# GpSimd adds the shared unit's softmax weights to each head's sums; one of four rounds of denominator products is left out

## The chip, the cores and the metric

The kernel runs on one core of a Trainium2 chip. The metric is the device time in microseconds (us); of several runs the median is given. Engines are named as the profile names them: PE is TensorE (matrix products), PEld its weight loads, DVE is VectorE, ACT is ScalarE, POOL is GpSimd, SP is SyncE, which here only issues loads.

## What is computed

Attention over 8 batches and 12 heads of 448 tokens and 64 columns, with a soft cap on the scores, and behind it a layer of 8 experts, of which each token uses one.

```python
scores = scale * np.matmul(q, k.transpose(0, 1, 3, 2))
scores = cap * np.tanh(scores / cap)
scores = scores - np.max(scores, axis=-1, keepdims=True)
attn = np.exp(scores)
attn = attn / (np.sum(attn, axis=-1, keepdims=True) + 1e-09)
x = np.matmul(attn, v)            # then heads side by side: 3584 tokens x 768
...
logits = x @ w_gate + modality_bias[modality_id]
e_idx = np.argmax(logits, axis=1)
...
h = np.maximum(x[mask] @ w1[e], 0.0)
out[mask] = gate_w[mask, None] * (h @ w2[e])
```

## The kernel before

**Pairs and units.** The heads of a batch are taken two at a time: 6 pairs a batch, 48 pairs in all, numbered g = 0 to 47. The 448 keys of each head are cut into three units of 128 keys of its own and a rest of 64. The rests of the two heads share one more unit, in which head 0 has partitions 0 to 63 and head 1 partitions 64 to 127. So a pair has 2 x 3 own units, whose softmax weights are the tile `pt` (128 keys by 6 by 448 queries), and one shared unit, whose weights are the tile `sh` (128 by 448). Keys stand on the partitions, queries along the row.

**One iteration.** `attention` runs g from 0 to 48. An iteration computes the scores of pair g in four steps (`scores`, L452, three products for each unit out of `hi` and `lo`, the two parts of the keys and queries that `prep` makes on DVE), ACT makes tanh (`th`, L454) and exponential (`pt` or `sh`, L456) out of them. In step 1, for pair g - 1: DVE adds the three own units of each head into `tot` (128 by 2 heads by 448; L555 and L556), and PE multiplies the own units with the values into `xT` (`weigh_own`, L461). In step 3 the shared unit's product (`weigh_shared`, L466) closes `xT`, and DVE copies it out of PSUM (L588). There is one `xT` buffer in PSUM, so `weigh_own` of the next iteration waits for that copy. The order on PE, and that of most DVE work, is the order in which the program is written; PE and DVE take one instruction after another.

**Denominators and gate logits.** Three pairs make a group h (`HB` = 3, 16 groups). The sum over keys, which is the denominator of the softmax, is itself a product: `sums` (L476) multiplies with the constant `pick`, which has a column of ones at row `GE` + j for head j. For each group it runs in four parts of three products each, all into one PSUM tile `glog`, with 32 rows for each pair:

| part | right-hand side | weights | what it adds |
|---|---|---|---|
| 0 | `tot` of head 0 | `pick[:, 0]` | the own keys of head 0 |
| 1 | `tot` of head 1 | `pick[:, 1]` | the own keys of head 1 |
| 2 | `sh` | `pick[:, 2]` | the shared unit, partitions 0 to 63 for head 0 and 64 to 127 for head 1 |
| 3 | `xT` copy | `wgt` | the unnormalized gate logits |

With r = (g - 4) mod 3, parts 0 and 1 run in the iterations with r = 0 (g = 4, 7, ... 46), parts 2 and 3 in those with r = 1 (g = 5, 8, ... 47), both in step 1 behind `weigh_own`; the last group's four parts run after the loop. Then DVE copies `glog` to `gl` (L480), PE turns it (`lt`, L488), and DVE divides (`logits`, L493 and L496). After every second group a batch is complete, and `route` picks each token's expert: DVE operations from L210 on, two small products in the next iteration (r = 2), then `rows` (L244, L247), `posf` and `pos` on DVE, and four indirect DMAs on POOL that put each token into the map `mapd` (L264).

**POOL.** GpSimd issues the stores of finished rows (`xd`, L517), those puts, the loads of the map (`mt`, L659) and the gathers of rows for an expert (`xg`, L666), and it has a small IOTA (`pay`, L255) that waits for the puts of the batch before to land. It does all of this in one queue, in order.

**The hand-over.** From g = 46 on the first expert's weights come in, and in the last iteration the first gathered rows (`xg`) are turned on PE (`ptr`, L702) in between. Behind the attention the products of the experts (L729 to L758) fill PE to the end.

**Buffers.** `tot` and `sh` have five buffers each (`HB + 2`), `pt` two.

Of the kernel before, what the change touches and what calls it, by code (L numbers as in the profile page):

```python
# [39 lines left out]
F32 = mybir.dt.float32  # L40
# [4 lines left out]
ALU = mybir.AluOpType  # L45
# [6 lines left out]
NP = H // 2  # L52
# [6 lines left out]
GW = 32  # L59
# [16 lines left out]
class Program:  # L76
# [7 lines left out]
    def pin(self, inst):  # L84
        return self.tc.keep_in_program_order(inst)
# [13 lines left out]
    def constants(self, cpool, dram):  # L99
        nc = self.nc  # L100
        self.xd = dram.tile([NT, DM], F32, name="xd")
        self.mapd = dram.tile([E * RG + W, 2], F32, name="mapd")
        self.metad = dram.tile([128, 4], I32, name="metad")

        self.ident = cpool.tile([128, 128], F32, name="ident")
        make_identity(nc, self.ident)
        self.identr = cpool.tile([128, 128], F32R, name="identr")
        nc.vector.tensor_copy(self.identr, self.ident)
        self.capt = cpool.tile([128, 1], F32, name="capt")
        nc.scalar.dma_start(self.capt, self.cap.unsqueeze(0).to_broadcast([128, 1]))  # L110
        self.flag = cpool.tile([1, 1], I32, name="flag")
        nc.vector.tensor_scalar(self.flag, self.capt[0:1], self.capt[0:1], CAP_FAST * CAP_FAST, op0=ALU.mult, op1=ALU.is_gt)
        self.cabs = cpool.tile([128, 1], F32, name="cabs")
        nc.vector.scalar_tensor_tensor(self.cabs, self.capt, -1.0, self.capt, op0=ALU.mult, op1=ALU.max)
        self.isc = cpool.tile([128, 1], F32, name="isc")
        nc.vector.reciprocal(self.isc, self.cabs)
        nc.vector.tensor_scalar(self.isc, self.isc, 0.125, None, op0=ALU.mult)


        act = cpool.tile([128, 1], F32, name="act")  # L120
        nc.scalar.activation(act, self.ident[:, 0:1], AF.Tanh)


        self.pick = cpool.tile([128, 3, GW], F32, name="pick")
        nc.vector.memset(self.pick, 0.0)
        for j in range(2):
            nc.vector.memset(self.pick[:, j, GE + j : GE + j + 1], 1.0)
            nc.vector.memset(self.pick[j * KR : (j + 1) * KR, 2, GE + j : GE + j + 1], 1.0)
        self.ones = cpool.tile([CP, 512], BF16, name="ones")
        nc.vector.memset(self.ones, 1.0)  # L130
        self.tri = cpool.tile([CP, CP], BF16, name="tri")
        nc.gpsimd.affine_select(
            self.tri, self.ones[:, :CP], pattern=[[1, CP]], compare_op=ALU.is_gt, fill=0.0, base=0, channel_multiplier=-1
        )
        self.desc = cpool.tile([128, E], F32, name="desc")
        nc.gpsimd.iota(self.desc, pattern=[[-1, E]], base=E, channel_multiplier=0, allow_small_or_imprecise_dtypes=True)
        self.region = cpool.tile([128, E], F32, name="region")
        nc.gpsimd.iota(self.region, pattern=[[RG, E]], base=0, channel_multiplier=0, allow_small_or_imprecise_dtypes=True)

        def table(name, shape, pattern, base=0, channel=0):  # L140
            t = cpool.tile(shape, F32, name=name)
            nc.gpsimd.iota(
                t, pattern=pattern, base=base, channel_multiplier=channel, allow_small_or_imprecise_dtypes=True
            )
            return t

        self.blkj = table("blkj", [128, E, RB], [[0, E], [1, RB]])
        self.blkr = table("blkr", [128, E, RB], [[RG, E], [W, RB]])
        self.blke = table("blke", [128, E, RB + 1], [[1, E], [0, RB + 1]])
        self.exp = table("exp", [128, E], [[1, E]])  # L150
        self.slot = table("slot", [128, 1], [[0, 1]], channel=1)

        self.acc = cpool.tile([CP, E], BF16, name="acc")
        nc.gpsimd.memset(self.acc, 0.0)
# [258 lines left out]
    def attention(self, qk, first, rp):  # L413
        tc, nc = self.tc, self.nc
        pe, pin = nc.tensor, self.pin
        with ExitStack() as st:
# [51 lines left out]
            def sums(h, part):  # L468

                if part == 0:  # L470
                    self.glog = ps_g.tile([128, 512], F32, name="glog")
                for t in range(HB):
                    xs_, tot, sh = kept[h * HB + t]
                    w = self.pick[:, part] if part < 3 else self.wgt[:, (h * HB + t) % NP]
                    rhs = (tot[:, 0], tot[:, 1], sh, xs_)[part]
                    pin(pe.matmul(self.glog[t * GW : (t + 1) * GW, :S], w, rhs, start=part == 0, stop=part == 3))  # L476

            def copy_sums():
                gl = xp.tile([HB * GW, S], F32, name="gl")
# [60 lines left out]
            for g in range(NG + 1):  # L540
# [4 lines left out]
                for step in range(C):  # L545
                    if step % 2 == 0 and g < NG:
                        scores(step, pt, sh, *cur[:2])
                        scores(step + 1, pt, sh, *cur[:2])
                    if step == 1:
                        if g + 1 < NG:  # L550
                            ready = prep(g + 1)
                        if g:
                            ppt, psh, pva = pend
                            tot = xp.tile([128, 2, S], F32, name="tot", bufs=HB + 2)
                            pin(nc.vector.tensor_tensor(tot, ppt[:, 0:2], ppt[:, 2:4], op=ALU.add))  # L555
                            pin(nc.vector.tensor_tensor(tot, tot, ppt[:, 4:6], op=ALU.add))  # L556
                            xT = ps_x.tile([128, 512], F32, name="xT")
                            weigh_own(xT, ppt, pva)

                        if g > HB:  # L560
                            h, r = divmod(g - HB - 1, HB)
                            if r < 2:
                                sums(h, 2 * r)
                                sums(h, 2 * r + 1)
                                if r:
                                    gl = copy_sums()
                    if step == 3:
                        if g in routing:
                            next(routing.pop(g), None)
                        if g == 3:  # L570
                            self.empty_map()
                        if g == 2:
                            self.gate_bias()

                        h, t = divmod(g - 2 * HB, HB)
                        if h >= 0 and (t == 0 or h < LAST):
                            if t == 0:
                                rec, xs = recs.pop(h), xp.tile([CP, C, HB * 128], F32, name="xs")
                            for u in (t,) if h < LAST else range(HB):
                                rows_out(h, u, xs, rec, h >= LAST)  # L580
                            if t == HB - 1 or h >= LAST:
                                store(h, xs)
                            if h == LAST:
                                meta = self.early_slot(self.cpool, self.ps_r)
                        if g:
                            weigh_shared(xT, psh, pva)
                            xs_ = xp.tile([128, S], F32, name="xT", bufs=2 * HB + 1)
                            pin(nc.vector.tensor_copy(xs_, xT[:, :S]))  # L588
                            kept[g - 1] = xs_, tot, psh
                        fetch(g + 2)  # L590
                        h, r = divmod(g - HB - 1, HB)
                        if h >= 0 and r == 1:
                            b = h // NH
                            if h % NH == 0:
                                lgs[b] = xp.tile([CP, C, H, E], F32, name="lg")
                            recs[h] = logits(h, by_token(gl), lgs[b])
                            if h % NH == NH - 1:
                                way = self.route(b, lgs[b], rp, self.ps_r)
                                next(way)
                                routing[g + 1] = way  # L600
                    for k in SPLITS.get((g, step), ()):
                        self.split_w(raws[k], self.w1s[k], pin=True)
                        if len(raws) < KC:
                            raws.append(self.load_raw(e, self.w1, len(raws), FF))
                    for k in MOVES.get((g, step), ()):
                        self.transpose(k, (ps_s, self.ps_r)[k % 2], ("sc", "small")[k % 2], busy=k < 2)
# [6 lines left out]
                    self.gather(early[1], known=NT - S)  # L613
            self.raws = [self.load_raw(e, self.w2, k, DM) for k in range(self.nstage)]
            h = NG // HB - 1
            for part in range(4):
                sums(h, part)
            rec = logits(h, by_token(copy_sums()), lgs[B - 1])
            way = self.route(B - 1, lgs[B - 1], rp, self.ps_r)
# [422 lines left out]
```

## Time and profile before

| | |
|---|---|
| median of three runs | 957.08 us (954.23 to 959.16) |
| the profiled execution | 955.14 us, its span 953.5 us |
| the attention | to about 421 us, at some 8 us a pair |
| the hand-over | some 400 to 425 us |
| products `glog` (L476), records x mean | `tot` 192 x 548 ns, `sh` 96 x 550 ns, `xT` 96 x 539 ns |
| additions for `tot` on DVE (L555, L556) | 48 x 1084 ns, 48 x 1092 ns |
| POOL busy | 131.6 us, 145 instructions |

One float32 product shows as two records on PE, so a part of `sums` (three products) shows as six. Records of neighbouring products overlap, so how long PE is taken is read from one start to the next. A row of the order of time has the start, the duration, the engine, the line, the operation with its tiles, and in brackets how long the engine stood idle ahead of it and for whom. A row of a group has the busy time in all and the mean of one in ns, then the idle time ahead of them. A row of a stage has the stage, its length, each engine's busy time, the granted clock and the DMA share.

### The profile page before, as it was taken

How to read it: one execution, taken by the hardware profiler on the slowest of the kernel's cores; microseconds unless marked ns; L12 is line 12 of the kernel's file. 1: busy time of each engine (PE TensorE's matmuls, PEld its weight loads, DVE VectorE, ACT ScalarE, POOL GpSimd, SP SyncE). 2: the span in 40 equal slices, each digit the busy share in tenths (PEclk: the TensorE clock that was granted, in tenths of full speed). 3: DMA queues.
4: the chain of work that ended last, by engine and by line, in shares of the span. 5: the costliest groups of instructions: out<-in, count | busy, mean ns of one | idle time of the engine just before them, and what ended most of it. 6: DMA issues, size and time to landing. Idle time of an engine off the chain costs nothing. (4 is left out here: it accounts for less than half of the span.)

```text
span 953.5 us, 14508 instructions
## 1 busy us (share of the span) xinstructions
PE 903.4 (95%) x5360; PEld 699.5 (73%) x5360; DVE 549.4 (58%) x940; ACT 558.5 (59%) x759; POOL 131.6 (14%) x145
## 2 busy tenths in 40 slices
PE   7999999999999999678899999999999999999997
PEld 3444445454545454258899999999999999998986
DVE  4777777777777778466444253343444443429662
ACT  6998888888888887603344343342444444336551
POOL 2002020202020202202420202020010202020100
PEclk9999999999999999978999999999999999999998
DMA  3433444453436343823863535455463635237660
GB/s 120 121 106 105 135 113 134 115 135 114 133 116 126 124 124 133 214 64 96 265 200 123 189 126 179 152 164 201 144 221 128 230 112 185 103 125 262 220 208 8
DMA packets 47178, 140.01 MB, mean 147 GB/s; under 512 B 8686, under 2 KB 9198, under 8 KB 47088
## 3 DMA queue, kind: packets, MB, share of 16 engines
q1 hardware_dynamic: 38000, 105.78, 36.2%
q0 software_dynamic: 8944, 33.10, 10.3%
q8 instruction: 47, 0.77, 0.3%
q14 instruction: 43, 0.35, 0.1%
q10 hardware_dynamic: 144, 0.00, 0.0%
HBM read 117.35 MB, written 22.69 MB: 147 GB/s over the span
## 5 line engine op out<-in xcount | busy, mean ns | idle before, releaser
L454 ACT ACTIVATE th<-sc,isc 128x896 f32<-128x896 f32 x192 | 168.7, 908 | 54.2 <-PE sc L452 54.1
L733 PE MATMUL ph<-x,al 128*128 128x384 f32 (+2 forms) x528 | 167.2, 317 | 0.0
L758 PE MATMUL py<-bh,hh 128*128 128x384 f32 x464 | 159.8, 344 | 4.3 <-ACT hh L739 4.3
L758 PE MATMUL py<-bl,hh 128*128 128x384 f32 x464 | 156.3, 337 | 0.0
L758 PE MATMUL py<-bh,hl 128*128 128x384 f32 x464 | 156.1, 337 | 0.0
L456 ACT ACTIVATE pt<-th,cabs 128x896 f32<-128x896 f32 x144 | 149.5, 1044 | 2.7
L729 PE MATMUL ph<-x,ah 128*128 128x384 f32 x384 | 129.9, 338 | 1.5 <-DVE hl L740 1.5
L730 PE MATMUL ph<-x,ah 128*128 128x384 f32 x384 | 129.0, 336 | 0.0
L461 PE MATMUL xT<-pt,va 128*64 128x448 f32 x576 | 119.7, 551 | 8.7 <-DVE xT L588 7.1
L683 DVE TENSOR_TENSOR bl<-raw,bh 128x768 fp32r<-128x768 f32 x88 | 81.3, 955 | 58.2 <-ACT bh L682 55.7
L682 ACT CAST bh<-raw 128x768 fp32r<-128x768 f32 x88 | 70.3, 839 | 68.0 <-DMA raw<-in_w_dram 55.3
L733 PEld LDWEIGHTS ph<-x,al 128*128 128x128 f32 x528 | 101.0, 191 | 0.0
L683 DVE TENSOR_TENSOR al<-raw,ah 128x1024 fp32r<-128x1024 f32 x66 | 78.8, 1222 | 27.8 <-ACT ah L682 27.3
L452 PEld LDWEIGHTS sc<-hi 64*128 64x128 f32 (+1 forms) x336 | 36.5, 187 | 77.7 <-ACT th L454 25.9
L763 ACT ACTIVATE ot<-py,mt 128x384 f32<-128x384 f32 x58 | 33.7, 581 | 99.2 <-PE py L758 51.8
L758 PEld LDWEIGHTS py<-bh,hh 128*128 128x128 f32 x464 | 87.8, 189 | 5.0 <-ACT hh L739 4.9
L712 DVE TENSOR_TENSOR x<-ptr,x 128x384 fp32r<-128x384 f32 (+2 forms) x66 | 32.7, 517 | 100.1 <-ACT x L711 97.0
L452 PE MATMUL sc<-hi 64*128 64x448 f32 (+1 forms) x336 | 86.9, 446 | 2.7 <-ACT th L454 2.1
L461 PEld LDWEIGHTS xT<-pt,va 128*64 128x64 f32 x576 | 37.5, 137 | 69.2 <-issue 45.4
L758 PEld LDWEIGHTS py<-bl,hh 128*128 128x128 f32 x464 | 87.9, 189 | 0.0
L758 PEld LDWEIGHTS py<-bh,hl 128*128 128x128 f32 x464 | 87.7, 189 | 0.1
L739 ACT ACTIVATE hh<-ph 128x384 fp32r<-128x384 f32 x64 | 30.4, 489 | 94.4 <-PE ph L733 94.4
(159 smaller groups left out, 1349.5 us busy)
## 6 DMA issues: line engine op xcount, KB each, us to landing
raw<-in_w_dram SPq DMA_DIRECT2D x66, 512.0 KB, 5.5
raw<-in_w_dram SPq DMA_DIRECT2D x88, 384.0 KB, 4.7
kq<-in_kq_dram SPq DMA_DIRECT2D x47, 480.0 KB
va<-in_v_dram SPq DMA_DIRECT2D x48, 256.0 KB, 2.9
xd<-xs POOLq DMA_DIRECT2D x16, 672.0 KB
mapd<-pay,pos POOLq DMA_INDIRECT x32
xg<-xd,mt POOLq DMA_INDIRECT x30
out_dram<-ot,mt POOLq DMA_INDIRECT x29
```

Source lines behind the costliest of these rows:

```text
L452: pin(pe.matmul(sc[:, j, :S], k[rows, ks], q[rows, KC2:], start=i == 0, stop=i == 2))
L454: nc.scalar.activation(th[:, :n], sc[:, :n, :S], AF.Tanh, scale=self.isc)
L456: nc.scalar.activation(dst, th[:, :n] if step < KU else th[:, 0], AF.Exp, scale=self.cabs)
L461: pin(pe.matmul(xT[j * D : (j + 1) * D, :S], va[:, u * D : (u + 1) * D], pt[:, u], start=u < 2, stop=False))
L682: a = self.nc.scalar.copy(hi, raw)
L683: b = self.nc.vector.tensor_tensor(lo, raw, hi, op=ALU.subtract)
L712: nc.vector.tensor_tensor(lo, pt[:, :w], hi, op=ALU.subtract)
L729: nc.tensor.matmul(ph[:, :w], hi[:, fs], self.x[:, k, 0, :w], start=first, stop=False)
L730: nc.tensor.matmul(ph[:, :w], hi[:, fs], self.x[:, k, 1, :w], start=False, stop=False)
L733: nc.tensor.matmul(ph[:, :w], lo[:, fs], self.x[:, k, 0, :w], start=False, stop=last)
L758: nc.tensor.matmul(py[:, :HALF], self.h[a][:, f, rows], self.w2s[f][c][:, cs], start=i == 0, stop=i == 3 * FC - 1,)
L763: nc.scalar.mul(ot[:, cs], py[:, :HALF], mt[:, t, 1:2])
```

## The change

The shared unit's weights are added into `tot` by GpSimd, head by head, on the partitions that belong to the head: two additions of 64 partitions by 448 for each pair, behind DVE's two. Part 2 of `sums` goes away with its part of `pick`; parts are now 0 and 1 (`tot`) and 2 (`xT`).

```diff
-        self.pick = cpool.tile([128, 3, GW], F32, name="pick")
+        self.pick = cpool.tile([128, 2, GW], F32, name="pick")
         nc.vector.memset(self.pick, 0.0)
         for j in range(2):
             nc.vector.memset(self.pick[:, j, GE + j : GE + j + 1], 1.0)
-            nc.vector.memset(self.pick[j * KR : (j + 1) * KR, 2, GE + j : GE + j + 1], 1.0)
...
-                    xs_, tot, sh = kept[h * HB + t]
-                    w = self.pick[:, part] if part < 3 else self.wgt[:, (h * HB + t) % NP]
-                    rhs = (tot[:, 0], tot[:, 1], sh, xs_)[part]
-                    pin(pe.matmul(self.glog[t * GW : (t + 1) * GW, :S], w, rhs, start=part == 0, stop=part == 3))
+                    xs_, tot = kept[h * HB + t]
+                    w = self.pick[:, part] if part < 2 else self.wgt[:, (h * HB + t) % NP]
+                    rhs = (tot[:, 0], tot[:, 1], xs_)[part]
+                    pin(pe.matmul(self.glog[t * GW : (t + 1) * GW, :S], w, rhs, start=part == 0, stop=part == 2))
...
                             pin(nc.vector.tensor_tensor(tot, tot, ppt[:, 4:6], op=ALU.add))
+                            for j in range(2):
+                                rows = slice(j * KR, (j + 1) * KR)
+                                nc.gpsimd.tensor_tensor(tot[rows, j], tot[rows, j], psh[rows], op=ALU.add)
...
-                                sums(h, 2 * r)
-                                sums(h, 2 * r + 1)
+                                for part in ((0, 1), (2,))[r]:
+                                    sums(h, part)
...
-                            kept[g - 1] = xs_, tot, psh
+                            kept[g - 1] = xs_, tot
...
-            for part in range(4):
+            for part in range(3):
                 sums(h, part)
```

On PE, in an iteration with r = 1, these rows stood in a row before (the scores of two steps, the own units' products, the two parts of `sums`, the next scores):

```order
L452 MATMUL sc<-lo,hi 128x448 x2
L461 MATMUL xT<-pt,va 64x448 x6
L476 MATMUL glog<-sh,pick 32x448 x3
L476 MATMUL glog<-xT,wgt 32x448 x3
L452 MATMUL sc<-hi 128x448 x2
```
And now:

```order
L451 MATMUL sc<-lo,hi 128x448 x2
L460 MATMUL xT<-pt,va 64x448 x6
L475 MATMUL glog<-xT,wgt 32x448 x3
L451 MATMUL sc<-hi 128x448 x2
L451 MATMUL sc<-hi,lo 128x448 x2
```
Three products are gone, here and in each of the 16 groups; nothing else on PE has moved. The orders on ACT and SP are the same, and that on DVE but for the memsets of `pick` at the start.

On POOL, around the puts of two batches, before (stores of rows `xd`, puts `mapd`, the IOTA that waits for the puts to land):

```order
L264 DMA mapd<-pay,pos 31104x2 x4
L255 IOTA pay 112x4
L517 DMA xd<-xs 448x1x384 x2
L264 DMA mapd<-pay,pos 31104x2 x4
L255 IOTA pay 112x4
```
And now, from the second store to the one after the IOTA:

```order
L516 DMA xd<-xs 448x1x384
L558 TENSOR_TENSOR tot<-tot,sh 64x448 x2
L263 DMA mapd<-pay,pos 31104x2 x4
L558 TENSOR_TENSOR tot<-tot,sh 64x448 x2
L254 IOTA pay 112x4
L558 TENSOR_TENSOR tot<-tot,sh 64x448 x2
L516 DMA xd<-xs 448x1x384
```
The last pair of a group is added ahead of the puts, the next two pairs behind them; the second addition of the first of these now carries the wait for the puts' landing that the IOTA had.

On POOL, at the hand-over, before (the load of the map for the first expert, its three gathers, the last two stores, the last puts):

```order
L659 DMA mt<-mapd 128x6
L255 IOTA pay 112x4
L666 DMA xg<-xd,mt 128x768 x3
L517 DMA xd<-xs 448x1x384 x2
L264 DMA mapd<-pay,pos 31104x2 x4
```
And now:

```order
L558 TENSOR_TENSOR tot<-tot,sh 64x448
L661 ISA
L661 DMA mt<-mapd 128x6
L558 TENSOR_TENSOR tot<-tot,sh 64x448
L254 IOTA pay 112x4
L668 DMA xg<-xd,mt 128x768 x3
L558 TENSOR_TENSOR tot<-tot,sh 64x448 x4
L516 DMA xd<-xs 448x1x384 x2
L263 DMA mapd<-pay,pos 31104x2 x4
```
One addition stands ahead of the map's load, one between load and gathers, and the last two pairs' four behind the gathers.

## The prediction

> **What bounds the kernel now.** I read the page's first part, then the busy time of each engine by stage, then the order of time inside one group of head pairs.
>
> ```profile
> span 953.5 us, 14508 instructions
> PE 903.4 (95%) x5360; PEld 699.5 (73%) x5360; DVE 549.4 (58%) x940; ACT 558.5 (59%) x759; POOL 131.6 (14%) x145
> ```
> ```profile
> core 0: us, PE busy (x) PEld busy (x) DVE busy (x) ACT busy (x) POOL busy (x), PEclk, DMA share, GB/s
> 140.00:240.00 100.00, 97.62 (x607) 49.56 (x608) 75.94 (x131) 86.36 (x103) 13.87 (x15) 1.00 0.44 119
> 400.00:425.00 25.00, 13.81 (x79) 9.31 (x80) 12.62 (x21) 2.06 (x5) 3.04 (x3) 0.66 0.39 132
> 600.00:950.00 350.00, 341.44 (x2031) 334.41 (x2029) 165.22 (x254) 148.94 (x245) 40.36 (x35) 1.00 0.49 164
> ```
> The change is all in the attention, and there PE is busy 97.6 us of 100 at a granted clock of 1.00; ACT has 86.4, DVE 75.9, POOL 13.9. Only the hand-over at 400 to 425 us has a large hole in PE. Behind it PE is at 97.6% again (341.44 of 350), so what the attention gains or loses arrives at the end whole. A busy PE is modelled, so whether PE really sets the pace is checked in the order of time, at an iteration that does the products in question (r = 1, once in three iterations):
>
> ```profile
> 167.29 1.09 DVE L556 TENSOR_TENSOR tot<-tot,pt 128x896 f32<-128x896 f32 x1
> 167.50 0.95 PE L476 MATMUL glog<-sh,pick 128*32 128x448 f32 x6
> 168.28 0.93 PE L476 MATMUL glog<-xT,wgt 128*32 128x448 f32 x6
> 169.27 0.62 DVE L480 COPY gl<-glog 96x448 f32<-96x448 f32 x1 [0.89 <-PE glog L476]
> 170.06 1.53 ACT L454 ACTIVATE th<-sc,isc 128x896 f32<-128x896 f32 x2 [1.29 <-PE sc L452]
> ```
> Behind these products ACT stands 1.29 us for the next scores and DVE 0.89 us for the finished sums. Both wait for PE. PE sets the pace here.
>
> **The part taken away.** Each round of `glog<-sh` is three products (six records). The round behind it starts 168.28 - 167.50 = 0.78 us later, so a round holds PE for 0.78 us; its records' own 0.95 overlap.
>
> ```profile
> L476 PE MATMUL glog<-sh,pick 128*32 128x448 f32 x96 | 15.2, 550 | 0.0
> ```
> 96 records are 16 rounds: one in each of the iterations g = 5, 8, ... 47, and one after the loop. ACT has 1.29 us in hand and DVE 0.89, both more than 0.78, so everything behind the round moves up by the whole 0.78. Fourteen rounds (g = 5 to 44) count: 14 x 0.78 = 10.9 us. The fifteenth (g = 47) does not, because PE soon stands in front of the first gathered rows, whose chain began earlier:
>
> ```profile
> 398.13 1.08 POOL L666 DMA_INDIRECT xg<-xd,mt  x1 [3.38 <-DMA mt<-mapd]
> 402.89 0.34 PE L702 MATMUL ptr<-identr,xg 128*128 128x128 f32 x1 [5.35 <-DMA xg<-xd,mt]
> 408.24 1.08 DVE L556 TENSOR_TENSOR tot<-tot,pt 128x896 f32<-128x896 f32 x1
> 418.57 1.89 PE L476 MATMUL glog<-tot,pick 128*32 128x448 f32 x12
> ```
> PE would only idle there 0.78 us longer than the 5.35 shown. The sixteenth, behind 418.57, stands in an unbroken run of PE and counts 0.78. Together **-11.7 us**. The smaller `pick` memset and the two dropped ones count nothing: DVE waits for loads behind them at the start.
>
> **The part added: its price.** 96 GpSimd additions, two for each of 48 pairs, 64 partitions by 448 with two SBUF inputs. The trace has no such operation. The nearest rows:
>
> ```profile
> L959 POOL MEMSET xg<- 128x2304 f32 x1 | 2.0, 2019 | 2.4 <-DVE identr L108 2.4
> masks.py:197 POOL MEMSET ident<- 128x128 f32 x1 | 0.2, 205 | 0.3 <-POOLq L1029 0.3
> masks.py:199 POOL TENSOR_SCALAR_AFFINE_SELECT ident<-ident 128x128 f32<-128x128 f32 x1 | 0.3, 283 | 0.0
> L142 POOL IOTA blke<- 128x88 f32 x1 | 0.4, 359 | 0.0
> L136 POOL IOTA desc<- 128x8 f32 x1 | 0.1, 133 | 0.0
> ```
> Below: writing alone costs (2019 - 205) / (2304 - 128) = 0.83 ns an element, so 448 take 205 + 320 x 0.83 = 0.47 us. Above: an IOTA grows by (359 - 133) / 80 = 2.8 ns an element, so 448 take 133 + 440 x 2.8 = 1.37 us. The AFFINE_SELECT, which reads one SBUF input, is the nearest: 78 ns more than the MEMSET of its size, 0.61 ns for each element read. Two inputs of 448 are 0.55 us more, so I take 0.47 + 0.55 = **1.02 us** an addition, 2.04 a pair.
>
> The Trainium skill (GPSIMD Engine Reference, Elementwise — side-by-side cycle accounting) gives some 2.6 cycles of 1.2 GHz an element, an estimate of 0.97 us here, and its section Engine selection advises against GpSimd for such sums; the sum below by it would be 0.4 us lower. No run here shows it yet.
>
> **Its place on POOL.** The additions run as soon as `tot` and `sh` are ready, and PE reads them in the next r = 0 iteration at the earliest. The tightest pair and the one delayed most:
>
> ```profile
> 135.77 1.70 PE L476 MATMUL glog<-tot,pick 128*32 128x448 f32 x12
> 179.21 1.09 DVE L556 TENSOR_TENSOR tot<-tot,pt 128x896 f32<-128x896 f32 x1
> 180.22 0.18 DVE L244 TENSOR_TENSOR rows<-rank,region 112x32 f32<-112x32 f32 x1
> 180.32 0.68 DVE L508 TENSOR_TENSOR xs<-tp,rec 112x512 f32<-112x512 f32 x1
> 180.92 0.18 DVE L247 TENSOR_TENSOR rows<-rows,oh 112x32 f32<-112x32 f32 x1
> 181.02 0.61 DVE L588 COPY xT<-xT 128x448 f32<-128x448 f32 x1
> 181.69 2.48 PE L461 MATMUL xT<-pt,va 128*64 128x448 f32 x12 [1.19 <-DVE xT L588]
> 184.09 1.70 PE L476 MATMUL glog<-tot,pick 128*32 128x448 f32 x12
> 196.74 0.13 POOL L255 IOTA pay<- 112x4 int32 x1 [7.63 <-DMA mapd<-pay,pos]
> 207.57 1.70 PE L476 MATMUL glog<-tot,pick 128*32 128x448 f32 x12
> ```
> `tot` is done at 179.21 + 1.09 = 180.30, PE's product comes at 184.09: 3.8 us for two additions of 1.02. Then four map puts and the wait for their landing hold POOL's queue to 196.74; one addition stands ahead of that wait, three remain behind it with the store. At 1.02 each they are done by some 201 us and the next pair's by 205, ahead of 207.57. At the end the `mt` load and the gathers stand behind one or two additions, but there POOL waits 3.38 us for `mt` anyway, and the last pair (`tot` done at 409.32, so some 412 with its additions) is wanted at 418.57. So POOL itself costs nothing on the path; at 1.9 us an addition the tightest pair would begin to.
>
> **Its cost on DVE.** GpSimd and VectorE get in each other's way:
>
> ```profile
> 5.56 2.02 POOL L959 MEMSET xg<- 128x2304 f32 x1 [2.39 <-DVE identr L108]
> 5.87 1.99 DVE L440 CAST hi<-kq 128x512 fp32r<-128x512 f32 x1 [0.45 <-issue]
> 7.52 0.48 POOL L171 MEMSET pre<- 128x120 f32 x1
> L440 DVE CAST hi<-kq 128x960 fp32r<-128x960 f32 x47 | 30.6, 652 | 6.6 <-DMA kq<-in_kq_dram 6.5
> 184.66 1.09 DVE L556 TENSOR_TENSOR tot<-tot,pt 128x896 f32<-128x896 f32 x1
> 184.73 1.89 POOL L264 DMA_INDIRECT mapd<-pay,pos  x1 [0.30 <-issue]
> 186.92 0.94 POOL L264 DMA_INDIRECT mapd<-pay,pos  x1 [0.30 <-issue]
> ```
> A cast of 960 elements takes 0.65 us, but one of 512 took 1.99, ending (7.86) just behind the memset that ran beside it (7.58) and ahead of the end of POOL's next. A put that takes 0.94 alone took 1.89 beside a `tot` addition. So one engine waits for the other's running instruction, then takes its turn ahead of the next one. The Trainium skill (SBUF — State Buffer, Who interferes with whom) words it as an exclusive lock on a port pair that the two share, taken by VectorE operations with two SBUF inputs or in a two-port mode but not by those that read PSUM and at most one SBUF input; the 1.99 and the 1.89 agree with it.
>
> In the ordinary iterations DVE, behind `tot`, turns to `gl`, `xs` and `xT`, which read PSUM, or stands idle, so little meets. What does meet is `hi` and `lo` of the next pair: up to 1 us late, with DVE idle time ahead of the next `xs`. I cost that at nothing; without that cover it would be up to 1.02 us in each.
>
> It is different in the seven iterations with a route (r = 2 behind each second group; the rows at 179 to 182 above). DVE is there without a gap, and PE already waits 1.19 us for `xT`, so a delay of DVE is a delay of PE. `tot` ends at 180.30, the first addition would run from about 180.37 to 181.39, and L247, with both inputs in SBUF, stands ahead of `xT` and wants to start at 180.92. It waits 0.47 us, then takes its turn ahead of the second addition. 7 x 0.47 = **+3.3 us**. By the bounds: nothing at 0.47 us an addition (done at 180.84); at 1.37, with both additions first, 180.37 + 2.74 - 180.92 = 2.2 us, so 15.3 in all.
>
> **Sum.** -11.7 + 3.3 = -8.4 us. The profiled execution took 955.14 us (1.6 around its span), so 946.7; the median of the three runs, 957.08, stands 1.94 higher, so **948.7 us** is the forecast.
>
> **Rivals.**
> *The additions cost DVE nothing* (a wake-up of POOL over 0.6 us after `tot`, or no conflict with so small an operation as L247). Here is how soon POOL starts behind the DVE operation that it waits for:
>
> ```profile
> 171.30 0.69 DVE L508 TENSOR_TENSOR xs<-tp,rec 112x512 f32<-112x512 f32 x1 [1.41 <-PE tp L507]
> 172.29 0.71 POOL L517 DMA_DIRECT2D xd<-xs  x1 [22.76 <-DVE xs L508]
> ```
> A store starts 0.30 us behind `xs` (171.99), so the wake-up would have to be twice that. -11.7: 945.4 us.
> *Both additions go ahead of L247.* The queued second addition keeps the port: 180.37 + 2.04 - 180.92 = 1.49 us, seven times 10.4, net -1.3: 955.8 us. Against it: the cast ended before POOL's second memset did.
> *Only half of the freed PE time arrives*, because ACT at 86% fills up. Against it: ACT's 1.29 us in hand. Half of 10.9 lost: 954.1 us.
> *DVE becomes the bound, and the kernel slower.* Six iterations take 184.09 - 135.77 = 48.32 us, 8.05 each, and DVE works 0.759 x 8.05 = 6.11 us in each. If an addition of h us held DVE for its whole length in each iteration, its time would be 6.11 + 2h. That passes 8.05 at h = 0.97; at 1.02 it gives 48 x 0.10 = +4.8 (961.9 us), at 1.37 +38 (995 us). Against it: the additions follow `tot`, where DVE reads PSUM or idles.
>
> **Chances and range.** Forecast 0.50, no DVE cost 0.22, both ahead 0.15, half lost 0.08, DVE-bound 0.05. A measurement of this kernel tells about 0.5% (4.8 us) from no change. Below 952.3 lie nearly all of the first two and a little of the others: faster 0.73, same 0.22, slower 0.05. The range 944 to 957 holds the first four but for their tails; the forecast's own is 946 to 951.5.
>
> **What would show it.** Right: PE's `glog<-xT` directly behind the own products in r = 1, ACT's wait there near 0.5 us instead of 1.29, three iterations 0.78 us shorter; L247 lengthened from 0.18 to some 0.65 and PE's wait for `xT` in route iterations from 1.19 to some 1.7; POOL some 98 us busier. Wrong: `xT` or `xs` late in ordinary iterations, PE waiting for POOL at `glog<-tot`, additions much over 1.4 us, or a longer hole at 400 us.

## The result, and the profile after

The changed kernel took 969.55 us (median; 966.88 to 969.6), the kernel before 956.65 us on the same chip: a ratio of 1.0121, with an interval of 1.0094 to 1.0149. It is slower by some 12 us, where 8 us faster was forecast. One further run, of 2035 us, stands far from the others and is left out.

The profiled execution took 969.5 us. The first part of its page, with busy times and counts of each engine:

```profile
span 967.9 us, 14527 instructions
PE 899.4 (93%) x5264; PEld 697.9 (72%) x5264; DVE 569.0 (59%) x938; ACT 558.8 (58%) x759; POOL 244.6 (25%) x241
```

PE is busy 4 us less only, although sixteen rounds of some 0.78 us are gone: other records of it took longer (the clock, below). The span is 14.4 us longer, so PE also waits more. The same stretches as before, by engine:

```profile
core 0: us, PE busy (x) PEld busy (x) DVE busy (x) ACT busy (x) POOL busy (x), PEclk, DMA share, GB/s
140.00:240.00 100.00, 89.81 (x545) 46.21 (x539) 74.19 (x119) 80.87 (x96) 39.34 (x37) 0.97 0.44 115
400.00:425.00 25.00, 9.43 (x51) 5.15 (x49) 15.38 (x20) 12.15 (x15) 11.22 (x10) 0.74 0.62 164
```

In the attention PE falls from 97.62 to 89.81 us of 100, and its mean granted clock from 1.00 to 0.97. What PE waits for there is told by the list of waits (in total, times, longest), of the changed kernel and then of the kernel before:

```profile
PE xT L460 <- DVE xT L590: 22.4, 12, 6.9
```
```profile
PE xT L461 <- DVE xT L588: 7.1, 6, 1.2
```

The groups of instructions show the products behind those waits (busy, mean ns of one), in the same order:

```profile
L460 PE MATMUL xT<-pt,va 128*64 128x448 f32 x576 | 126.2, 576 | 24.4 <-DVE xT L590 22.4 <-ACT th L453 2.0
```
```profile
L461 PE MATMUL xT<-pt,va 128*64 128x448 f32 x576 | 119.7, 551 | 8.7 <-DVE xT L588 7.1 <-ACT th L454 1.6
```

Before, PE waited six times 1.2 us for the copy of `xT`, once behind each route; now twelve times, up to 6.9 us. That is 15.3 us more. The same 576 records also take 6.5 us longer. That is the clock: 5.0 us of it in three places of the kind shown below, and 1.5 at the start, where the granted clock is 0.50 from 19.7 to 22.6 us and was 1.00 before. The freed rounds are there: in each of the 14 iterations g = 5, 8, ... 44 the period from its `xT<-pt,va` to the next is 0.73 to 0.79 us shorter than before, 10.6 us in all. So 15.3 + 6.5 - 10.6 = +11.2 us, and the 48th `xT<-pt,va` does begin 11.24 us later than before. This place, called **pair 48** below, is the yardstick of the experiments; pair 25 is the 25th `xT<-pt,va`, and so on.

The same 11.2 us by place, period by period against before: the freed rounds -10.6; the six periods behind routes +3.4; the periods that end at pairs 13, 25, 31 and 43, each behind a batch's map puts, +10.2 (0.8, 6.9, 1.2 and 1.4); three windows of halved clock, ahead of pairs 17, 26 and 35, +5.0; the first three periods +2.9; the last three +0.3.

The other 3.2 us arise behind it, in the hand-over and the experts; no experiment went after them.

An ordinary r = 1 iteration looks as forecast, with ACT's wait at 0.54 instead of 1.29:

```profile
170.00 1.09 DVE L555 TENSOR_TENSOR tot<-tot,pt 128x896 f32<-128x896 f32 x1
170.23 0.95 PE L475 MATMUL glog<-xT,wgt 128*32 128x448 f32 x6
172.03 1.53 ACT L453 ACTIVATE th<-sc,isc 128x896 f32<-128x896 f32 x2 [0.54 <-PE sc L451]
```

**The route iteration.** The order of time at the first addition behind a `tot` of a route:

```profile
133.37 2.34 POOL L558 TENSOR_TENSOR tot<-tot,sh 64x448 f32<-64x448 f32 x2 [7.47 <-DVE rows L243]
133.81 0.73 DVE L246 TENSOR_TENSOR rows<-rows,oh 112x32 f32<-112x32 f32 x1
134.47 0.61 DVE L590 COPY xT<-xT 128x448 f32<-128x448 f32 x1
135.13 4.17 PE L460 MATMUL xT<-pt,va 128*64 128x448 f32 x12 [1.75 <-DVE xT L590]
```

`rows` takes 0.73 instead of 0.18, PE waits 1.75 instead of 1.19, and then its twelve products take 4.17 instead of 2.48 us. The last is new. Four consecutive stretches of 3.41 us around it, same columns as above (the granted clock is the number behind POOL):

```profile
128.48:131.89 3.41, 3.41 (x21) 1.83 (x17) 3.31 (x10) 3.38 (x5) 0.00 (x0) 1.00 0.13 46
131.89:135.30 3.41, 1.66 (x15) 1.22 (x16) 3.41 (x9) 3.38 (x5) 1.86 (x2) 1.00 0.68 223
135.30:138.71 3.41, 3.41 (x10) 1.00 (x10) 3.31 (x6) 1.84 (x2) 1.69 (x3) 0.50 0.16 21
138.71:142.12 3.41, 3.41 (x24) 1.32 (x21) 0.92 (x1) 0.34 (x1) 2.80 (x3) 1.00 0.35 129
```

The clock is set in windows of 3.41 us: where PE was busy only 1.66 us of one, the whole next window ran at 0.50, and PE lost 1.7 us.

**The store.** The largest loss, 6.9 us at pair 25, in order of time:

```profile
197.91 0.69 DVE L507 TENSOR_TENSOR xs<-tp,rec 112x512 f32<-112x512 f32 x1 [0.65 <-PE tp L506]
...
201.49 1.14 POOL L558 TENSOR_TENSOR tot<-tot,sh 64x448 f32<-64x448 f32 x1 [7.98 <-DMA mapd<-pay,pos]
...
201.81 1.33 DVE L439 CAST hi<-kq 128x960 fp32r<-128x960 f32 x1 [1.86 <-DMA kq<-in_kq_dram]
...
203.27 4.03 POOL L558 TENSOR_TENSOR tot<-tot,sh 64x448 f32<-64x448 f32 x2
204.26 2.03 DVE L554 TENSOR_TENSOR tot<-pt 128x896 f32<-128x896 f32 x1
206.39 1.86 DVE L555 TENSOR_TENSOR tot<-tot,pt 128x896 f32<-128x896 f32 x1
207.24 0.71 POOL L516 DMA_DIRECT2D xd<-xs  x1
...
212.56 0.69 DVE L507 TENSOR_TENSOR xs<-tp,rec 112x512 f32<-112x512 f32 x1 [4.32 <-DMA xd<-xs]
...
213.84 4.13 PE L460 MATMUL xT<-pt,va 128*64 128x448 f32 x12 [6.85 <-DVE xT L590]
```

The second addition behind the puts waits 7.98 us for their landing. Three additions then run nearly in a row and meet DVE's `hi`, which takes 1.33 instead of 0.65, and `tot`, which takes 2.03 and 1.86 instead of 1.09. DVE is late by itself there, too: `hi` waits 1.86 us for the load of `kq` (before: 0.34). The store of `xs`, complete at 198.60, stands behind them in POOL's queue and leaves at 207.24 (before: 0.3 us behind `xs`). There is one `xs` buffer, so the next `xs` waits 4.32 us for the store to land; behind it on DVE stands the copy of `xT`, and behind that PE.

### The profile page after: what moved, and what is told of

Read it like the earlier page. It is cut to its first block, busy times and chain, and to the rows that moved or that the text cites. A ratio compares the mean times of both kernels' runs of the same rounds, so it can differ in the third digit from the quotient of the medians.

```text
span 967.9 us, 14527 instructions
## 1 busy us (share of the span) xinstructions
PE 899.4 (93%) x5264; PEld 697.9 (72%) x5264; DVE 569.0 (59%) x938; ACT 558.8 (58%) x759; POOL 244.6 (25%) x241
## 5 line engine op out<-in xcount | busy, mean ns | idle before, releaser
L558 POOL TENSOR_TENSOR tot<-tot,sh 64x448 f32<-64x448 f32 x96 | 114.0, 1188 | 219.7 <-DVE tot L555 82.0
L460 PE MATMUL xT<-pt,va 128*64 128x448 f32 x576 | 126.2, 576 | 24.4 <-DVE xT L590 22.4
L770 POOL DMA_INDIRECT out_dram<-ot,mt x29 | 31.8, 1097 | 389.2 <-ACT ot L765 307.4
```

What stands on the lines that cost most here:

```text
L460: pin(pe.matmul(xT[j * D : (j + 1) * D, :S], va[:, u * D : (u + 1) * D], pt[:, u], start=u < 2, stop=False))
L558: nc.gpsimd.tensor_tensor(tot[rows, j], tot[rows, j], psh[rows], op=ALU.add)
```

## The experiments

Each row gives the medians of the kernel and of the kernel before, measured on the same chip, their ratio with its interval, and two readings of the profiled execution against that of before: the start of pair 48 and PE's waits for `xT` in total.

| run | us | before | ratio | pair 48 | waits |
|---|---|---|---|---|---|
| changed kernel | 969.55 | 956.65 | 1.0121 [1.0094, 1.0149] | +11.2 | 22.4 |
| e1 without additions | 947.79 | 956.18 | 0.9916 [0.9883, 0.9949] | -10.5 | 7.1 |
| e2 additions only | 962.73 | 956.18 | 1.0056 [1.0031, 1.0081] | +12.1 | 18.2 |
| e4 `rows` in PSUM | 975.99 | 956.18 | 1.0176 [1.0114, 1.0237] | +19.8 | 27.5 |
| e5 two `xs` buffers | 956.14 | 956.18 | 1.0009 [0.9979, 1.0039] | -1.3 | 13.3 |
| e8 both | 955.98 | 956.28 | 0.9997 [0.9961, 1.0032] | -0.8 | 13.8 |
| e9 store on SP | 1019.61 | 956.28 | 1.0659 [1.0633, 1.0685] | +63.9 | 27.9 |
| e7 additions on DVE | 960.97 | 956.28 | 1.0052 [1.0024, 1.0081] | +2.7 | 16.9 |
| e10 the same, later | 962.08 | 956.28 | 1.0049 [1.001, 1.0087] | +4.8 | 13.6 |
| e11 some pairs on PE | 958.55 | 957.46 | 1.0036 [1.0013, 1.006] | +4.4 | 11.9 |
| e12 other pairs on PE | 953.57 | 957.46 | 0.9973 [0.9953, 0.9992] | +2.2 | 10.2 |
| e13 fourth block | 949.94 | 956.87 | 0.9943 [0.9922, 0.9964] | -4.7 | 7.4 |
| e14 groups on PE | 952.02 | 956.87 | 0.9948 [0.993, 0.9967] | -0.6 | 8.9 |

### e1 and e2: each half alone

e1 is the changed kernel without these lines, e2 the kernel before with them:

```diff
-                            for j in range(2):
-                                rows = slice(j * KR, (j + 1) * KR)
-                                nc.gpsimd.tensor_tensor(tot[rows, j], tot[rows, j], psh[rows], op=ALU.add)
```

> The changed kernel without the GpSimd additions: the denominators lack the shared unit's weights. Theory (the freed PE rounds pay as forecast; everything lost comes with the additions): 14 x 0.76 = 10.6 us from the loop and about 0.8 behind it, so about 11 to 12 us faster than before, some 945 us, and the clock records of the attention between 20 and 370 us stay at full speed. Rival (the freed time goes elsewhere, or the shorter PE work itself lets the clock fall): clearly less than 8 us faster, with drops of the clock that before does not have.

> The kernel before with the additions put in, nothing taken out: the shared unit counts twice in the denominators. Theory (the additions cost by themselves what the changed kernel lost against my forecast of the freed rounds): +12 and +11 to 12 from the first run, so about 23 us slower than before, some 978 to 981 us, with the wait for the xd store in front of xs and drops of the clock at the route iterations. Rival (part of the loss comes from the loop's shorter iterations, which leave POOL less time): 12 to 18 us slower.

In e1 the denominators lack the shared unit's weights, but each engine has as many instructions as in the changed kernel, except for the additions. All 14 periods are shorter by 0.75 to 0.78 us, no other period of the first 44 differs by more than 0.26, no window of halved clock lies between 20 and 365 us, and pair 48 begins 10.5 us earlier. So the freed rounds pay as forecast. At the first products `py` of the experts the lead is 13.1 us, at the end of the span 8.2: behind 839 us PE waits 1.88 us for "issue" (for nothing that the profile shows) and has a halved window that the profiled execution of before has not. That part was not tried further.

e2 chose other experts for its tokens (its doubled weights change the logits) and had fewer instructions behind the attention (880 on DVE in all instead of 940), so its time can't be used; pair 48 can. There the additions cost 12.1 us, with the theory's waits for the store (six, at most 1.6 us) but without one halved window. In the changed kernel they cost 11.2 + 10.6 = 21.8. The first theory, that they cost by themselves what was lost, falls: 9.7 us arise only together with the shorter iterations of PE. Most of that lies in the one wait at pair 25 (6.9 us against 1.6) and in the halved windows ahead of pairs 17, 26 and 35 (5.0 us).

### e4, e5 and e8: the route's product and the store

e4 keeps `rows` in the PSUM tile of `rank`; e5 gives `xs` two buffers (and `tot` and `sh` one and two fewer, to fit); e8 does both:

```diff
-        rows = pool.tile([CP, C, E], F32, name="rows")
+        rows = rk.rearrange("p (c e) -> p c e", c=C)
...
-                                rec, xs = recs.pop(h), xp.tile([CP, C, HB * 128], F32, name="xs")
+                                rec, xs = recs.pop(h), xp.tile([CP, C, HB * 128], F32, name="xs", bufs=2)
```

> The changed kernel with the route's rows kept in the PSUM bank of rank, so that the product with oh has one SBUF input and one in PSUM. Theory (that product waits for the first addition because both of its inputs are in SBUF, and the later xT copy makes PE wait 1.75 instead of 1.2 us, which halves its clock): the product's mean back from about 670 to under 300 ns, 6 x 0.55 = 3.3 us gained and the two dips of 1.7 us at pairs 17 and 35 gone, about 5 to 7 us faster than the changed kernel. Rival (any DVE operation beside an addition waits, wherever its inputs are): no difference.

> The changed kernel with two xs buffers in place of one (tot and sh have fewer, to fit). Theory (the xd store is queued on POOL behind additions that wait for the puts' landing, and the next xs waits for the store): DVE's waits for the xd store are gone, PE's wait of 6.85 us at pair 25 and of 1.1 us at pair 31 shrink below 1 us, and the dip of the clock behind the first is gone: 7 to 10 us faster than the changed kernel. Rival (those waits come from additions that hold VectorE's operations back, whatever buffers there are): under 3 us.

> The changed kernel with both edits: rows in PSUM and two xs buffers. Theory (three costs add up: the route's product behind an addition, the xs that waits for the late store, and the clock windows that the longer PE waits set off; the rows edit alone lost because the store's wait, whose length varies, was still there): no wait of PE above 1.3 us between 30 and 365 us, no window of halved clock there, pair 48 begins 7 to 9 us earlier than before, 947 to 952 us. Rival (with the route's product out of the way the waits turn up at another place): pair 48 within 4 us of before, 953 us or more.

e4's product reads PSUM and one SBUF tile, and runs beside the same additions without a delay:

```profile
133.73 2.84 POOL L558 TENSOR_TENSOR tot<-tot,sh 64x448 f32<-64x448 f32 x2 [7.47 <-DVE rank L243]
134.18 0.18 DVE L246 TENSOR_TENSOR rank<-rank,oh 112x32 f32<-112x32 f32 x1
134.27 0.61 DVE L590 COPY xT<-xT 128x448 f32<-128x448 f32 x1
134.94 1.35 PE L460 MATMUL xT<-pt,va 128*64 128x448 f32 x6 [1.18 <-DVE xT L590]
```

The six periods behind routes are within 0.03 us of before, where the changed kernel lost 0.55 to 0.59 in each. So the mechanism of the route's term is shown. The time, however, was not 5 to 7 us better: its interval overlaps that of the changed kernel, and in the profiled execution, the slowest of the four, pair 48 begins 8.6 us later. DVE's waits for the store grew to 16.1 us in six places (5.8 in two before this edit), and PE lost 6.3 us at pair 25 and 6.6 at pair 37. This edit does not touch the store.

e5 takes DVE's waits for `xd` away altogether, and against the changed kernel it gains 1.0121 - 1.0009 = 1.1%, some 10.7 us. The route's 0.55 us stay, as they should. Pair 25 loses nothing in its profiled execution, but that is not the buffer's doing alone: the puts landed early there, as the table below shows. It has one halved window (1.7 us) up to 365 us in place of three, so the gain is that of the waits and of the windows together.

e8 should have added both gains and did not: 955.98, the rival's range. Its waits sit where the puts have just landed:

```profile
197.14 1.14 POOL L558 TENSOR_TENSOR tot<-tot,sh 64x448 f32<-64x448 f32 x1 [6.78 <-DMA mapd<-pay,pos]
...
197.46 1.34 DVE L439 CAST hi<-kq 128x960 fp32r<-128x960 f32 x1 [1.72 <-DMA kq<-in_kq_dram]
...
198.92 4.04 POOL L558 TENSOR_TENSOR tot<-tot,sh 64x448 f32<-64x448 f32 x2
199.91 2.03 DVE L554 TENSOR_TENSOR tot<-pt 128x896 f32<-128x896 f32 x1
202.04 1.86 DVE L555 TENSOR_TENSOR tot<-tot,pt 128x896 f32<-128x896 f32 x1
...
205.09 1.35 PE L460 MATMUL xT<-pt,va 128*64 128x448 f32 x6 [2.30 <-DVE xT L590]
```

Here no store is waited for. The bunched additions lengthen `hi` to 1.34 us and the two parts of `tot` to 2.03 and 1.86, and `hi` itself starts 1.72 us late for its load. Together they make `xs` and `xT` late, and PE waits 2.3 us; how much each does is not separated.

The traces show what the difference between the kernels goes with. The table has, for two of the pairs behind a batch's puts, the time from the end of the last put to the start of the operation that waits for their landing, the time from the end of `xs` to its store, and by how much PE's period is longer than before, in us:

| run | pair 25: landing | store | PE | pair 37: landing | store | PE |
|---|---|---|---|---|---|---|
| before | 7.6 | 0.3 | | 7.8 | 0.7 | |
| changed kernel | 9.4 | 8.6 | 6.9 | 5.1 | 0.7 | 0.0 |
| e4, one `xs` | 9.2 | 8.9 | 6.3 | 8.4 | 8.4 | 6.6 |
| e8, two `xs` | 8.7 | 8.5 | 2.4 | 8.9 | 8.7 | 2.5 |
| e5, two `xs` | 4.7 | 0.7 | 0.0 | 7.4 | 4.9 | 1.0 |

Without additions the store leaves at once behind a landing of 7.6 or 7.8 us. With them, where the landing takes 8.4 us or more, the store leaves 8 to 9 us late and PE loses time; where it takes 5.1 or less, PE loses nothing. e4 and e8 are the fair pair, since they differ in the buffers alone and their stores are equally late: with two buffers PE loses some 4 us less at each place. Pair 48 begins 20.6 us earlier in e8 than in e4, halved windows included. The landing differs between executions and places, and the five late ones of the table come with a `hi` that waits 1.7 to 2.5 us for its load. What makes them late was not tried.

### e9: the store on another queue

```diff
-                nc.gpsimd.dma_start(
+                nc.sync.dma_start(
```

> The changed kernel with the xd store issued from SyncE's queue in place of GpSimd's; one xs buffer, as in the changed kernel. Theory (the store is late because it stands on POOL behind additions that wait for the puts' landing): the store leaves within 1 us of its xs, DVE never waits for it, pair 25 loses nothing, and the time is that of the two-buffer kernel, 953 to 959 us. Rival (the store's landing is late by itself, through contention of its transfer): the waits for xd stay, 965 us or more.

DVE no longer waits for the store, as the theory had it, but neither theory saw the price. SP also issues the loads of `kq` and `va`, and now holds them until `xs` is done: its queue waits 111.2 us in all for `xs`. In the list of waits DVE's `hi`, which waited 6.5 us in all for its load before, waits ten times as long:

```profile
DVE hi L439 <- DMA kq<-in_kq_dram: 64.8, 17, 8.1
```

### e7 and e10: the additions on VectorE

e7 has them behind `tot`, e10 behind the copy of `xT`:

```diff
+                                pin(nc.vector.tensor_tensor(tot[rows, j], tot[rows, j], psh[rows], op=ALU.add))
```

> The changed kernel with the additions on VectorE, directly behind tot. GpSimd is out of it. Theory: nothing in ordinary iterations, since VectorE has about 1.9 us free in each and an addition should take some 0.55; in the six route iterations xT is 1.1 us late, PE waits about 2.3 us, more than half of a clock window, and three or more of them halve the clock for 1.7 us: -11 + 6.6 + 5 to 10, so 956 to 961 us. Rival (the clock falls for other reasons than the wait's length): no halved windows, -11 + 6.6, 951 to 953 us.

> The same additions on VectorE, but behind the copy of xT. Theory: they delay no xT; the next pair's hi and lo, some 1.1 us later, are still in time for the scores, so all the freed PE time arrives as in the kernel without additions: 945 to 949 us. Rival (VectorE's order has no 1.1 us to spare there: logits, hi and lo come late in every iteration or in every third): 953 us or more.

An addition takes 0.62 us on DVE. In e7 each route iteration costs 1.40 us (PE waits 2.58), more than the 1.1 expected, and only one wait brings a halved window there, where three or more were expected; that the time lies just within the theory's range is in part luck. e10's theory falls: the copy of `xT` is no longer behind its own pair's additions, but DVE works without a gap from the logits of the iteration before through the route, so 1.24 us put in there arrive at the next `xT`: 1.24 to 1.28 us in each of six, and four halved windows. DVE has time to spare on the average, and none around a route.

### e11, e12 and e14: some pairs stay on PE

All three keep `sh` and the fourth round for the pairs of `on_pe` and add the others on GpSimd. The condition shown is e11's; e12 has `p % 6 in (2, 3)`, e14 `p < HB or p // HB % 2 == 1`. e11 and e14 have `rows` in PSUM, and all have one `xs` buffer.

```diff
+            def on_pe(p):
+                return p < 3 or p % 6 == 3
...
+                    if part == 2 and not on_pe(h * HB + t):
+                        continue
```

> The changed kernel with the shared unit's product back on PE for the pairs whose additions would stand behind the map puts (the first pair after each route, p % 6 == 3) and for the first three pairs, beside the loads of the bias; the other 38 pairs stay with GpSimd. Rows in PSUM; one xs buffer. Theory (what is left of the loss comes from additions that POOL holds back until the puts have landed: they bunch up, meet lo and tot on VectorE and make the store and xs late): without them in that place no wait of PE for xT above 1.3 us between 30 and 365 us although xs has one buffer, and 7 x 0.51 + 6 x 0.76 = 8.1 us of freed PE time arrive, so pair 48 begins 7 to 9 us earlier than before and the time is 947 to 951 us. Rival (the additions of the second pair after the route, or the store by itself, still come late): waits of 2 us or more stay at pairs 25, 37 or 43, 953 us or more.

> As the run before, but by place alone: the product is on PE for the pair of each route iteration and for the pair behind it (p % 6 in 2, 3), GpSimd has the other 32; rows stays in SBUF. Theory (each cost of the additions sits in one of these two iterations): the route's product with oh is back at about 0.18 us, PE waits there 1.2 us, no window of halved clock between 30 and 365 us, 14 x 0.51 = 7.1 us arrive, 948 to 952 us. Rival (additions cost something in every iteration): pair 48 begins less than 4 us earlier than before, 953 us or more.

> The changed kernel with whole groups of three pairs on the one or the other: the first group and every second one, behind whose start the map puts land, keep the PE round; GpSimd adds for the other seven; rows in PSUM, one xs buffer. Theory (a PE round of one pair costs a whole round, and the additions do harm only behind the puts' landing): 6 x 0.76 = 4.6 us arrive, no wait of PE above 1.3 us between 30 and 365 us, 950 to 953 us. Rival (additions cost elsewhere too, by the store or by lo and tot): waits as at pair 25 stay, 955 us or more.

e11 still loses 3.5 us at pair 25, although no addition carries the wait for the landing. One pair's additions between the landing and the store are enough to make the store 5.7 us late (there, too, the load of `kq` is 1.9 us late):

```profile
197.45 0.13 POOL L255 IOTA pay<- 112x4 int32 x1 [8.89 <-DMA mapd<-pay,pos]
197.66 2.66 POOL L564 TENSOR_TENSOR tot<-tot,sh 64x448 f32<-64x448 f32 x2
...
200.26 0.72 POOL L522 DMA_DIRECT2D xd<-xs  x1
...
205.10 0.69 DVE L513 TENSOR_TENSOR xs<-tp,rec 112x512 f32<-112x512 f32 x1 [1.56 <-DMA xd<-xs]
```

And a group with one pair on PE saves nothing: its period is that of before to 0.05 us in e11 and e12, where I had expected 0.51 less; only e11's groups without any are 0.75 to 0.79 shorter. The rows of e12 show why:

```profile
169.40 0.56 PE L481 MATMUL glog<-sh,pick 128*32 128x448 f32 x1
169.41 0.57 PE L481 MATMUL glog<-xT,wgt 128*32 128x448 f32 x2
169.79 0.54 PE L481 MATMUL glog<-sh,pick 128*32 128x448 f32 x1
169.81 1.28 PE L481 MATMUL glog<-xT,wgt 128*32 128x448 f32 x4
```

Products into different blocks of 32 rows of PSUM begin within 0.02 us of each other and run side by side. A round of three costs what one product costs. e12 has the waits of before in its route iterations and no halved window from 20 to 365 us, but keeps a round in every group; it is 0.3% faster than before although pair 48 is 2.2 us later in its profiled execution. That execution has less halved clock between 30 and 945 us than that of before (23.9 us against 34.1); whether this is the gain was not tried. e14 leaves whole groups alone and is 0.5% faster; its six pure groups save 0.76 to 0.78 each, but 1.9 us go at pair 25 and 2.4 at pair 46, so its theory's "no wait" failed, although the time fell within its range.

### e13: the product moved beside others

With that, the shared unit needs no engine but PE. `glog` has a fourth block of 32 rows that is not used:

```diff
+                w, sh = self.half[:, 4 - 2 * part : GW + 4 - 2 * part], kept[h * HB + part][2]
+                pin(pe.matmul(self.glog[HB * GW :, :S], w, sh, start=part == 0, stop=part == 2))
...
-                    pin(pe.transpose(lt[:CP, c * w : (c + 1) * w], gl[:, c * CP : (c + 1) * CP], self.ident[:w, :w]))
+                    pin(pe.matmul(lt[:CP, c * w : (c + 1) * w], gl[:, c * CP : (c + 1) * CP], self.fold, start=True, stop=True))
```

> The kernel before, no additions anywhere. The two runs before this one showed that a round with the product of one pair holds PE as long as one with three, so the pairs' products, which go to 32 rows of PSUM each, seem to run side by side. Here the shared unit's product of pair t goes to the free fourth block of 32 rows of glog, beside one of the three other rounds, and the transposes by the identity become products with a matrix that also adds these six rows to the denominators. Theory (the fourth product runs beside the three others): 14 x 0.76 = 10.6 us arrive, pair 48 begins 10 to 11 us earlier than before as in the run without additions, some 945 to 949 us. Rival (four products take longer than three by a third of a round each): 3 x 0.26 is given back in each group, no gain, 955 to 958 us.

```profile
166.15 0.58 PE L484 MATMUL glog<-xT,wgt 128*32 128x448 f32 x3
166.17 0.56 PE L486 MATMUL glog<-sh,half 128*32 128x448 f32 x1
166.55 0.55 PE L484 MATMUL glog<-xT,wgt 128*32 128x448 f32 x3
166.57 0.54 PE L486 MATMUL glog<-sh,half 128*32 128x448 f32 x1
```

The fourth product does run beside the three. But the 14 periods are only 0.30 to 0.34 us shorter, not 0.76. The missing part is in the group of `lt`, of before and of e13:

```profile
L488 PE MATMUL lt<-ident,gl 96*112 96x96 f32 x64 | 7.9, 245 | 0.0
```
```profile
L498 PE MATMUL lt<-fold,gl 128*112 128x96 f32 x128 | 15.0, 261 | 0.2 <-DVE gl L490 0.2
```

As products, the four turns of `gl` in a group leave twice the records: (15.0 - 7.9) / 16 = 0.44 us more in each group. At 949.94 us, 0.9943 [0.9922, 0.9964], it has the lowest median of the kernels that compute everything, though e14's interval overlaps its own, and is some 2% under the changed one, with the waits of before (7.4 us) and no halved window up to 365 us.

## Why the prediction was wrong

- **What bounds the kernel: right.** e1's periods show PE's pace and nothing else.
- **-11.7 for the rounds: right in the attention.** 14 x 0.76 = 10.6 to pair 48, and in e1 12.0 at the `ptr` behind the last wait of the hand-over (400.71 against 412.72); the whole kernel kept 8.
- **1.02 us an addition: nearly.** 96 took 114.0 us, a mean of 1.19 and a median of 1.14. The estimate from the Trainium skill (GPSIMD Engine Reference, Elementwise — side-by-side cycle accounting), 0.97, was lower still. Its section Engine selection advises VectorE for such sums, some 2 times faster; the runs agree on the time (0.62 us on VectorE), but in e7 and e10 VectorE was not a good place either.

```profile
L558 POOL TENSOR_TENSOR tot<-tot,sh 64x448 f32<-64x448 f32 x96 | 114.0, 1188 | 219.7 <-DVE tot L555 82.0 <-DVE rows L243 52.1 <-PE glog L475 41.5
L246 DVE TENSOR_TENSOR rows<-rows,oh 112x32 f32<-112x32 f32 x8 | 5.4, 669 | 0.0
L440 DVE TENSOR_TENSOR lo<-kq,hi 128x960 fp32r<-128x960 f32 (+2 forms) x49 | 60.5, 1236 | 1.2
```

- **+3.3 for the routes: right in place and size.** Six periods lost 0.55 to 0.59 (forecast 0.47 in each of seven; with an addition of 1.14 the same sum gives 0.59), `rows` took 0.67 (forecast some 0.65), PE's wait was 1.75 (forecast some 1.7), and e4 removed it. The seventh lost 0.15 only, so that the total of 3.4 for 3.3 is in part luck. That e4's product has one input in PSUM and no delay agrees with the rule of the Trainium skill (SBUF — State Buffer, Who interferes with whom).
- **"So POOL itself costs nothing on the path": this step failed.** I checked whether the additions behind the puts' landing are done before `glog<-tot` wants them, and they are. I left out the other things that wait for that queue: the store behind the additions, the single `xs` buffer behind the store, and `xT` behind `xs` on DVE. I had even counted the store among what is "done by some 201 us"; it left at 207.24. The prediction's own sign of being wrong, `xs` late in an ordinary iteration, is what the trace has there. The puts had ended 2.9 us later than in the trace of before, their landing took 9.4 us behind them instead of 7.6, and two of the additions took 2.0 us each beside `tot` instead of 1.02. In place of nothing, the four pairs behind the puts cost 10.2 us, and a second `xs` buffer gained some 10.7 us over the whole kernel (e5).
- **`hi` and `lo` late "at nothing": failed where additions bunch.** One addition at a time does little (periods in ordinary iterations are unchanged). Three behind one another, let loose by the landing, lengthen `hi` by 0.7 us and both parts of `tot` by 0.9 and 0.8; with a late load of `kq` this makes e8's 2.3 us.
- **A missing term: the clock.** No step asked what a longer wait of PE does to the granted clock. In the changed kernel it cost 5.0 us in three places.
- **The start, also missing.** Beside the work for the bias two operations of DVE take 1.01 and 1.24 us instead of 0.18 and 0.42 while an addition runs, and PE waits 1.72 us; 1.5 to 1.9 us were lost at pair 3 with GpSimd additions in that place, none in e11 and e14, whose first group has none.
- **The rival that ended slower** (DVE becomes the bound, 961.9 us) had the sign and the wrong mechanism: DVE was not full, it was held back at a few places.

What stays open: why the puts land after 4 us at one place and after 9 at another, and whether the additions have a part in that; what share of the waits at pair 25 is the late load of `kq`; and the 3 to 5 us behind pair 48. The clock's part was read off the traces and not tried with a wait made on purpose.

## What to carry to other kernels

When work goes to an idle engine, list everything that already stands in that engine's queue, what of it waits for a transfer to land, and who waits for each; a mean of 14% busy says nothing about 8 us of standing still. Follow each buffer to its next writer: here one store behind a few additions stopped PE through a single buffer. And before moving a product off PE, see whether it fits beside one that is there.

## What the runs showed of the hardware

- **The clock falls in windows.** In all traces the stretches of halved clock begin on a grid of 3.41 us with a phase of its own in each execution. Between 30 and 365 us, a window at full clock in which PE stood idle up to 1.4 us was never followed by a halved one; behind 2.1 us or more it always was; from 1.5 to 2.0 us both were seen (1.51 in e10 halved the next, 1.95 in e7 did not). The six waits of 1.2 us before the change stayed below that. The Trainium skill (TensorE: Matmul & The Clock Gate, Part 1: The HAM clock gate) has a free-running window of some 3.4 us, with which the traces agree, and warns of a whole idle window; here about half of one was enough.
- **Products into different 32-row blocks of PSUM overlap**, four as well as three (starts 0.01 to 0.02 us apart in e12 and e13). The Trainium skill (the same page, Part 3: Packing small matmuls — row/col tiling) describes such a packing; the rows agree.
- **A GpSimd addition of 64 x 448 took 1.14 us, the same on VectorE 0.62.**
